# Lightning attention and a leaky-ReLU MLP on one core: the MLP begins on half a group of chunks, and one sum moves behind a drain

## The chip, the cores and the metric

The kernel runs on one core of a Trainium2 chip. A core has five engines with a queue each, which run beside one another and wait for one another through semaphores: TensorE (PE) multiplies matrices, VectorE (DVE), ScalarE (ACT) and GpSimd (POOL) work element by element, and SyncE (SP) issues the transfers. The metric is the time of the whole program on the device in microseconds; smaller is better.

## The reference

Two parts follow one another, all in float32 except the weights, which arrive as float64.

```python
for b in range(nb):                          # 12 blocks of 64 tokens, per batch (4) and head (8), head size 64
    intra = einsum('bhic,bhjc->bhij', qb, kb) * Dmask
    intra = einsum('bhij,bhjd->bhid', intra, vb)
    inter = einsum('bhid,bhde->bhie', qb * lam_pow, kv_state)
    out[:, :, sl] = intra + inter
    kv_state = lam_block * kv_state + einsum('bhsd,bhse->bhde', kb * rev_pow, vb)
...
x = out.transpose(0, 2, 1, 3).reshape(3072, 512)
h = x @ w_in                                 # 512 x 2048
g = maximum(0.01 * h, h)
return g @ w_out                             # 2048 x 512
```

The first part is attention with a decay per head: `intra` is what the tokens of a block give one another, `inter` is what the running state of all earlier blocks gives them. The second part is an MLP with a leaky ReLU.

## The kernel before

**Chunks.** Attention works on 24 chunks of 128 tokens (two blocks of 64). A chunk goes through `step()` (L473), which returns three parts; `c` is the new chunk and `b` the one before it:

1. `own(b)`: the `intra` rows of chunk `b` into the PSUM tile `po`; `inter(b, 0)`: half of its `inter` products, added in `po`.
2. `transpose_k`, `transpose_q` (L375, L382): PE transposes, ACT copies them out (L372), POOL multiplies the keys by their decay (L379), and the queries are multiplied as well, by DVE while the flag `alone` is set and by POOL later.
3. `scores(c)` into the PSUM tile `ps` (L391), `inter(b, 1)` (the other half), after which ACT writes chunk `b`, times 4, into the MLP's input `x` (L471); `kv(c)` and `sums_kv(c)` bring the state forward (L406, L422). While `alone` is set, `kv` uses the PSUM banks Z and W, later the banks of the transposes.

The two halves of `inter` are apart[...]; the scores stand between them.

**Groups and units.** Four chunks make a group of 512 tokens (six groups). The MLP works on a group in four units of 512 hidden columns: `up(g, u)` (L553) makes the hidden values, `down(g, u)` (L585) adds their share to the group's output `os`. Each is a product of 2 x 2 blocks done with seven multiplications instead of eight, in the manner of Strassen: `product` (L496) runs P1, P2, P6, P5, P7, P3, P4 in this order, alternately into the PSUM banks Z and W. Z stays open from P1 to P6, P7 and P4, W from P2 on: each bank gathers several products, and between them `keep` (L512: a copy on ACT, or an addition on DVE at L514 where the output already holds an earlier unit) and `total` (L518) drain it. A product that follows in a bank waits for that drain.

`PROD` (L491) says which blocks a product multiplies. A11 and A12 are the rows of a group's first two chunks, A21 and A22 those of its last two. S1 to S4 are sums of them: P6 uses S2, P5 S1, P7 S3 and P3 S4; P1 uses A11 and P2 A12 alone. `sums` (L535) makes them: for `x` of the first group on DVE, of later groups on POOL (`x_sums`, L545, called once all parts of a group's last `up` are out), and for the hidden values on DVE. There S1, S2, S3 are made at the end of `up` (L577), and S4 within `down`, after P2 has read A12, whose place it takes (L598). S3 takes the place of A21.

**Weights.** `conversion` (L244) turns each pair of float64 blocks into a float32 tile of seven slots, the four blocks and three differences T1, T2, T4 that the seven products need. ACT makes three passes for each block (L270, L281, L284), DVE two for a pair and one for each block (L289, L293, L298), and the differences (L305) are made by DVE or POOL, as `T_DVE` says by the pair's number. A raw block waits in the place of a weight tile that is not yet in use.

**What sets the order.** All engines' orders are written out by the Python program, which keeps a clock of its own per engine (`run`, L176), with a cost for each operation. Conversions stand in the lists `later` and are put into an engine's queue where the planned time has room for them (`emit`, L188); `need` (L199) forces those that the next unit requires. Loads are issued by SP in the order of the string `LOADS` (L160, `c` a chunk, `w` a weight block), as far as their places are free. `together(parts, n)` (L617) spreads the next `n` parts of attention over the products of a unit; the list `STEPS` has the `n` of each unit and `FIRST` how many parts run before the first one.

So before the first unit, 16 parts run: chunks 0 to 4 up to `own(4)` and its first half of `inter`.

Of the kernel before, what the change touches and what calls it, by code (L numbers as in the profile page):

```python
# [38 lines left out]
F32 = mybir.dt.float32  # L39
# [5 lines left out]
ALU = mybir.AluOpType  # L45
# [14 lines left out]
def kernel(  # L60
# [10 lines left out]
    nc = tc.nc  # L71
    P = 128
    B, H, S, D = q.shape
    C = P
    C2 = C // 2
    NCB = S // C
    HP = H // 2
    d_model, d_ff = moe_w_in.shape
    KO = d_model // P
    FO = d_ff // P  # L80
    NCH = B * NCB
    GC = 4
    NG = NCH // GC
# [4 lines left out]
    NU = NP // UP  # L88
# [68 lines left out]
    ROOMS = ["st"] + [f"{w}{p}" for w, p, h in reversed(blocks) if h == 0 and p >= UP]  # L157


    LOADS = "cwwcwwcwccccwwwcwwwccwwwwwwcwwwwwwwwwwwwwww" + "c" * NCH  # L160
    SLACK, AHEAD = (0.55, 0), (8.0, 14.0)

    T_DVE = [1, 3, 4, 9, 11, 14]

    FIRST, STEPS = 16, [4, 1, 2, 5, 6, 5, 3, 4, 0, 0, 0, 2, 0, 0, 0, 4]
    rooms = {}
    w_raw, lo, w_done = {}, {}, 0

# [7 lines left out]
    def run(eng, us, fn, after=(), gives=None, fill=True):  # L176
        t = max([ready.get(k, 0.0) for k in after], default=0.0)
        if fill and eng in later:
            while later[eng] and emit(eng, t + SLACK[alone]):
                pass  # L180
        clk[eng] = max(clk[eng], t) + us
        fn()
        if gives is not None:
            ready[gives] = clk[eng] + 0.1
        if eng != "DMA":
            pump()
# [22 lines left out]
    def pump(urgent=False):  # L209
        while urgent or clk["DMA"] < clk["PE"] + AHEAD[fin > 3]:  # L210
            able = [x for x in sorted(y[0] for y in loads.values() if y) if x[2]()]
            if not able:
                return
            loads[able[0][1]].pop(0)
            able[0][3]()
# [131 lines left out]
    def quad(out, rows, lhsT, rhs, cols, start=False):  # L347

        nc.tensor.matmul(out[HALF[cols]], lhsT=lhsT[HALF[rows]], rhs=rhs[HALF[rows]], start=start, stop=True,  # L351
                         skip_group_check=True)

    def tokens(t):
        return slice(t * C2, (t + 1) * C2)
# [94 lines left out]
        fin = b + 1  # L450
        ready["fin", b] = ready["own", b]

    def inter(b, n):


        def go():
            for i in range(HP):
                t = i % 2 ^ n
                for hi in range(2):
                    if b % NCB or t:  # L460
                        x, y = place(2 * i + hi)
                        quad(po[b][:, t, i, :], x, state[(2 * b + t - 1) % 4][:, y, :], qsT[b][:, y, tokens(t)], hi)

        run("PE", 0.3, go, [("qsT", b), ("state", 2 * b)], "inter")
        if n == 0:
            return
        g, r, t = b // GC, b % GC * C // T, b % GC * C % T
        if g not in X:
            X[g] = xp.tile([P, 2, 2, KO // 2, T], F32, name="x", tag="x", bufs=NX)
        x = X[g][:, r, :, :, t:t + C].rearrange("p h k (t i) -> p t (h k) i", t=2)  # L470
        run("ACT", 0.6, lambda: nc.scalar.mul(x, po.pop(b)[:, :, 0:HP, :], 4.0), ["inter"], ("x", b))  # L471

    def step():  # L473


        nonlocal at
        s, at = at, at + 1
        b, c = (x if 0 <= x < NCH else None for x in (s - 1, s))

        def has(x, *fs):  # L480
            for f in fs if x is not None else ():
                f(x)

        return [lambda: has(b, own, lambda b: inter(b, 0)),
                lambda: has(c, transpose_k, transpose_q),
                lambda: (has(c, scores), has(b, lambda b: inter(b, 1)), has(c, kv, sums_kv))]

    A = ("A11", "A12", "A21", "A22", "S1", "S2", "S3", "S4")  # L490
# [44 lines left out]
    def sums(eng, us, t, names, after):  # L535

        for o, a, b, op in (("S1", "A21", "A22", ALU.add), ("S2", "S1", "A11", ALU.subtract),
                            ("S3", "A11", "A21", ALU.subtract), ("S4", "A12", "S2", ALU.subtract)):
            if o in names:
                e = nc.vector if eng == "DVE" else nc.gpsimd  # L540
                run(eng, us, lambda: e.tensor_tensor(t[o], t[a], t[b], op=op), after, ("sum", eng, o))  # L541

    summed = set()

    def x_sums(g):  # L545
        summed.add(g)
        x = X[g]
        xs = xp.tile([P, 4, KO // 2, T], F32, name="xs", tag="xs")
        X[g] = {s: x[:, i // 2, i % 2] if i < 4 else xs[:, i - 4] for i, s in enumerate(A)}
        sums("DVE" if g == 0 else "POOL", 1.8 if g else 0.72, {s: x.rearrange("p k c -> p (k c)") for s, x in X[g].items()},  # L550
             A[4:], [("x", GC * g + GC - 1)])

    def up(g, u):  # L553
        q4 = ("A11", "A12", "A21", "A22")

        def begin():
            if g not in summed:
                x_sums(g)

            G[g, u] = {s: xp.tile([P, UP, T], F32, name=f"g{s}", tag=f"g{s}") for s in A[:6]}  # L560
            G[g, u].update(S3=G[g, u]["A21"], S4=G[g, u]["A12"])

        def mm(t, name, first):
            sa, sb = PROD[name]
            x = X[g][sa]
            for i in range(UP):
                w = WI[UP * u + i][:, SI[sb], :].rearrange("p (k f) -> p k f", k=2)
                for kk in range(2):
                    nc.tensor.matmul(t[:, i, :], lhsT=w[:, kk, :], rhs=x[:, kk, :],  # L569
                                     start=(first and i == 0 and kk == 0), stop=(i == UP - 1 and kk == 1),  # L570
                                     skip_group_check=True)

        def done(i):
            if i != 2:
                leaky(G[g, u][q4[i]], G[g, u][q4[i]], f"tot{i}", q4[i])
            else:
                sums("DVE", 0.72, G[g, u], ("S1", "S2", "S3"), ["A21", "A22", "A11"])  # L577

        parts = product(mm, 1.73, lambda i: G[g, u][q4[i]], lambda z: leaky(G[g, u]["A21"], z, "Z", "A21"), done,
                        lambda name: [("sum", "POOL" if g else "DVE", PROD[name][0]), ("x", GC * g + GC - 1)])  # L580
        return [lambda: (begin(), parts[0]())] + parts[1:]

    osb = {}
# [1 line left out]
    def down(g, u):  # L585
        def o(i):
            if g not in osb:
                osb[g] = tp.tile([P, GC, d_model], F32, name="os", tag="os", bufs=1)
            return osb[g][:, i // 2 * 2:i // 2 * 2 + 2, i % 2 * HD:(i % 2 + 1) * HD]

        def mm(t, name, first):
            sa, sb = PROD[name]
            for m in range(T // P):
                for i in range(UP):
                    nc.tensor.matmul(t[:, m, :], lhsT=G[g, u][sa][:, i, m * P:(m + 1) * P], rhs=WO[UP * u + i][:, SO[sb], :],  # L595
                                     start=(first and m == 0 and i == 0), stop=(i == UP - 1), skip_group_check=True)
            if name == "P2":
                sums("DVE", 0.72, G[g, u], ("S4",), ["W"])  # L598

        def put(z):  # L600
            if u == 0:
                run("ACT", 0.6, lambda: nc.scalar.copy(o(2), z), ["Z"])
            else:
                run("DVE", 0.72, lambda: nc.vector.tensor_tensor(o(2), o(2), z, op=ALU.add), ["Z"])

        def done(i):
            if u == NU - 1:
                rows = out[(g * GC + i // 2 * 2) * C:(g * GC + i // 2 * 2 + 2) * C, i % 2 * HD:(i % 2 + 1) * HD]
                nc.sync.dma_start(out=rows.rearrange("(m p) n -> p m n", p=P), in_=o(i))

        return product(mm, 1.73, o, put, done,
                       lambda name: [PROD[name][0], ("sum", "DVE", PROD[name][0])], u > 0)
# [4 lines left out]
    def together(parts, n):  # L617

        extra = []
        while len(extra) < n and (todo or at < NCH + 1):  # L620
            todo.extend([] if todo else step())
            extra.append(todo.pop(0))
        m = len(extra)
        for i, part in enumerate(parts):
            part()
            while m - len(extra) < m * (i + 1) // len(parts):
                extra.pop(0)()
        for x in extra:
            x()
# [4 lines left out]
    for i, x in enumerate(LOADS):  # L634
# [5 lines left out]
        else:  # L640
            loads[x].append((i, x, lambda n=n: room_free(n), lambda n=n: load_w(n)))
    pump()
    together([], FIRST)
    alone = False
    for n, (g, u, w) in enumerate((g, u, w) for g in range(NG) for u in range(NU) for w in range(2)):
        need((2 * u + w + 1) * NW // (2 * NU))
        together((up, down)[w](g, u), STEPS[n] if n < len(STEPS) else 3 * (w == 0))
        if (u, w) == (NU - 1, 0) and ("x", GC * g + 2 * GC - 1) in ready:
            x_sums(g + 1)

# [29 lines left out]
```

## Time and profile before

706.91 us, median of three runs (706.82 to 708.93). The profiled execution spans 707.5 us.

| engine | busy us | share of the span |
|---|---|---|
| PE (products) | 680.1 | 96% |
| PE (weight loads, beside the products) | 584.5 | 83% |
| DVE | 329.9 | 47% |
| ACT | 217.4 | 31% |
| POOL | 147.6 | 21% |

Where PE was not busy, us of each stretch:

| stretch | length | PE busy |
|---|---|---|
| 0 to 20 | 20.0 | 15.4 |
| 20 to 40 | 20.0 | 12.4 |
| 40 to 180 | 140.0 | 135.0 |
| 180 to 500 | 320.0 | 316.0 |
| 500 to 600 | 100.0 | 97.8 |
| 600 to 680 | 80.0 | 80.0 |
| 680 to 707.5 | 27.5 | 23.6 |

A line of a timeline gives start, duration, engine, source line, operation, output and inputs, number of instructions, and in brackets the idle time before it and what ended that. A product of the MLP shows as eight matrix instructions that start 1.73 us after those of the product before; it is drawn as 1.89 us long, since the ends overlap. In a line of windows, the busy time and number of instructions of PE, of its weight loads, of DVE, ACT and POOL follow one another, then the granted clock of PE (1.00 is full), the share of the DMA engines that was busy and what they moved.

### The profile page before, as it was taken

The numbers are of one execution on the slowest core, as the hardware profiler recorded it, in microseconds if no ns is written. First come the engines' busy times: TensorE is split into PE (matmuls) and PEld (weight loads), VectorE is DVE, ScalarE is ACT, GpSimd is POOL, SyncE is SP. The second block draws the span as 40 slices with busy tenths as digits, with TensorE's granted clock in tenths as the row PEclk, the third lists the DMA queues.
The fourth block names the chain that finished last, engine by engine and source line by source line (L and its number), as shares of the span: only waits on it lengthen the run. The fifth ranks groups of instructions, "written<-read, shape, count | busy, mean of one in ns | idle before, by whom it ended". The sixth has DMA issues, their size and how long they took to land.

```text
span 707.5 us, 13346 instructions
## 1 busy us (share of the span) xinstructions
PE 680.1 (96%) x5834; PEld 584.5 (83%) x5834; DVE 329.9 (47%) x488; ACT 217.4 (31%) x361; POOL 147.6 (21%) x141
## 2 busy tenths in 40 slices
PE   7689998999999999999999999999999998999997
PEld 5578777888888887888887888888888887888886
DVE  4768699876325325224245333343333244234324
ACT  4647767661221211321202223112122211221210
POOL 2741576557001004101205102103000003000000
PEclk9989999999999999999999999999999999999999
DMA  8998165643101003302202110000100000100001
GB/s 220 244 265 272 47 194 137 164 128 97 31 1 31 1 1 90 76 1 45 45 1 47 50 41 2 0 2 0 60 1 0 1 1 15 45 0 1 1 0 60
DMA packets 93130, 42.81 MB, mean 61 GB/s; under 512 B 76688, under 2 KB 91024, under 8 KB 93072
## 3 DMA queue, kind: packets, MB, share of 16 engines
q1 hardware_dynamic: 92928, 41.95, 22.5%
q8 instruction: 46, 0.75, 0.5%
q14 instruction: 12, 0.10, 0.0%
q10 hardware_dynamic: 144, 0.00, 0.0%
HBM read 35.66 MB, written 6.29 MB: 59 GB/s over the span
## 4 chain that ended last, share of the span: by engine, by line
PE 86%; DVE 6%; issue 2%; POOL 2%; ACT 1%; SPq 1%; DMA 1%; DVEq 0%; POOLq 0%; ACTq 0%
PE Z L595 23%; PE Z L569 23%; PE W L569 17%; PE W L595 16%; PE po L351 2%; PE pt L367 2%; PE ps L351 2%; DVE gS L541 2%; PE pu L351 1%; POOL state L433 1%; SPq L340 1%; POOL wi L305 1%; DMA q<-in_q_dram 1%; DVE state L430 1%; DVE os L514 1%
## 5 line engine op out<-in xcount | busy, mean ns | idle before, releaser
L595 PE MATMUL Z<-wo,gA 128*128 128x256 f32 x576 | 137.4, 381 | 0.0
L595 PEld LDWEIGHTS Z<-wo,gA 128*128 128x128 f32 x576 | 107.9, 190 | 14.8
L569 PE MATMUL Z<-x,wi 128*128 128x256 f32 x384 | 94.0, 387 | 1.1 <-DVE wi L298 0.5
L569 PE MATMUL Z<-xs,wi 128*128 128x256 f32 x384 | 91.3, 380 | 1.2 <-POOL wi L305 1.2
L569 PE MATMUL W<-xs,wi 128*128 128x256 f32 x384 | 91.7, 382 | 0.0
L516 ACT COPY gA<-Z 128x512 f32<-128x512 f32 x48 | 28.1, 585 | 206.5 <-PE Z L569 206.5
L595 PE MATMUL W<-wo,gA 128*128 128x256 f32 x384 | 90.8, 379 | 0.0
L569 PEld LDWEIGHTS Z<-x,wi 128*128 128x128 f32 x384 | 73.1, 193 | 12.3 <-DVE wi L298 1.4
L569 PEld LDWEIGHTS Z<-xs,wi 128*128 128x128 f32 x384 | 72.5, 190 | 11.4 <-POOL wi L305 1.6
L595 PEld LDWEIGHTS W<-wo,gA 128*128 128x128 f32 x384 | 72.8, 190 | 9.9
L569 PEld LDWEIGHTS W<-xs,wi 128*128 128x128 f32 x384 | 71.5, 190 | 9.6
L532 ACT ACTIVATE gA<-gA 128x512 f32<-128x512 f32 x72 | 45.3, 630 | 108.7 <-DVE gA L520 108.7
L520 DVE TENSOR_TENSOR gA<-gA,W 128x512 f32<-128x512 f32 x48 | 33.0, 688 | 88.0 <-PE W L569 84.6
L379 POOL TENSOR_TENSOR k<-k,decay 128x512 f32<-128x512 f32 (+1 forms) x24 | 27.2, 1133 | 216.0 <-PE pt L367 211.3
L520 DVE TENSOR_TENSOR gA<-gA,Z 128x512 f32<-128x512 f32 x24 | 16.5, 688 | 105.5 <-PE Z L569 105.5
L595 PE MATMUL Z<-wo,gS 128*128 128x256 f32 x192 | 48.3, 396 | 8.0 <-DVE os L514 8.0
L595 PEld LDWEIGHTS Z<-wo,gS 128*128 128x128 f32 x192 | 36.2, 194 | 16.3 <-DVE os L514 11.7
L541 POOL TENSOR_TENSOR xs<-x 128x512 f32<-128x512 f32 x10 | 14.9, 1493 | 156.0 <-PE W L569 156.0
L595 PE MATMUL W<-wo,gS 128*128 128x256 f32 x192 | 45.7, 381 | 0.0
L569 PE MATMUL W<-x,wi 128*128 128x256 f32 x192 | 45.6, 381 | 0.0
L433 POOL TENSOR_TENSOR state<-state,pow_q 128x256 f32<-128x256 f32 x40 | 30.8, 771 | 64.1 <-DVE state L430 44.7
L520 DVE TENSOR_TENSOR os<-os,W 128x512 f32<-128x512 f32 x48 | 32.8, 683 | 23.0 <-PE W L595 23.0
(76 smaller groups left out, 765.1 us busy)
## 6 DMA issues: line engine op xcount, KB each, us to landing
ws<-in_moe_w_in_dram SPq DMA_DIRECT2D x16, 512.0 KB, 5.5
ws<-in_moe_w_out_dram SPq DMA_DIRECT2D x16, 512.0 KB, 6.0
k<-in_k_dram SPq DMA_DIRECT2D x48, 128.0 KB, 4.1
q<-in_q_dram SPq DMA_DIRECT2D x48, 128.0 KB, 3.1
v<-in_v_dram SPq DMA_DIRECT2D x24, 256.0 KB, 4.0
out_dram<-os SPq DMA_DIRECT2D x24, 256.0 KB, 2.2
lam_b<-in_lam_dram ACTq DMA_DIRECT2D x1, 4.0 KB, 2.7
```

What stands on the lines that cost most here:

```text
L305: return lambda: e.tensor_tensor(*(W[p][:, s[i]:s[i] + m, :] for i in (out, a, b)), op=ALU.subtract)
L340: nc.sync.dma_start(out=x[:, i * HP:(i + 1) * HP, :], in_=y[i::2].rearrange("h p d -> p h d"))
L351: nc.tensor.matmul(out[HALF[cols]], lhsT=lhsT[HALF[rows]], rhs=rhs[HALF[rows]], start=start, stop=True, skip_group_check=True)
L367: nc.tensor.transpose(out=pt[:, y, :], in_=loaded[c][i][:, 2 * y:2 * y + 2, :].rearrange("p a d -> p (a d)"), identity=ident)
L379: run("POOL", 1.2, lambda: nc.gpsimd.tensor_tensor(kr[n], kr[n], _bc(pow_k, 3, D)[n], op=ALU.mult), [("pt", "k")], ("kd", c))
L433: run("POOL", 0.8, lambda: nc.gpsimd.tensor_tensor(state[(m + 1) % 4], new, _bc(lam_c, 2, D), op=ALU.mult), [("state", m)], ("lstate", m + 1))
L516: run("ACT", 0.6, lambda: nc.scalar.copy(dst(i), st[tag]), [tag], f"keep{i}")
L520: lambda: nc.vector.tensor_tensor(dst(i), dst(i), st[tag], op=ALU.add), [f"keep{i}", tag], f"tot{i}")
L532: run("ACT", 0.64, lambda: nc.scalar.activation(out=dst, in_=src, func=AF.Prelu, bias=0.0, scale=1.0, alpha=0.01), [after], gives)
L541: run(eng, us, lambda: e.tensor_tensor(t[o], t[a], t[b], op=op), after, ("sum", eng, o))
L569: nc.tensor.matmul(t[:, i, :], lhsT=w[:, kk, :], rhs=x[:, kk, :], start=(first and i == 0 and kk == 0), stop=(i == UP - 1 and kk == 1), sk ...
L595: nc.tensor.matmul(t[:, m, :], lhsT=G[g, u][sa][:, i, m * P:(m + 1) * P], rhs=WO[UP * u + i][:, SO[sb], :], start=(first and m == 0 and i ...
```

## The change

It has four parts.

- **The first unit begins on half a group.** P1 and P2 of the first `up` read the rows of chunks 0 and 1 alone. They now run between the parts of chunk 3: the program does nine parts, then takes three more one by one, with P1 behind chunk 3's transposes and P2 behind its scores and state. Both no longer wait for chunk 3's `x`. `FIRST` is 2 parts after this, where it was 16 in all. `alone` is cleared before chunk 3's `kv`, so that Z is free for P1.
- **Chunk 3's inter is made apart.** The sums of `x` need chunk 3 early. `early` runs `own(3)` and the first half of `inter` into `po`, and the second half at once into a tile in the place of the scores, `ps`, from which two additions on DVE bring it into `x`. So no scores of the next chunk need to stand between.
- **One sum of activations later.** S3 of the hidden values is made after P2 of `down` and the drain of its Z, with S4, and not at the end of `up`.
- **The last store in halves.** The last block of the output is added and stored in two halves.

With this go other values for the order of the loads (three weight blocks ahead of two chunks), for which differences DVE makes (pairs 0 and 7 join, 4 goes to POOL) and for how many parts of attention run beside each unit.

```diff
-    LOADS = "cwwcwwcwccccwwwcwwwccwwwwwwcwwwwwwwwwwwwwww" + "c" * NCH
+    LOADS = "cwwcwwcwccwwwcwwwccccwcwwwwwwwwwwwwwwwwwwww" + "c" * NCH
...
-    T_DVE = [1, 3, 4, 9, 11, 14]
+    T_DVE = [0, 1, 3, 7, 9, 11, 14]
-    FIRST, STEPS = 16, [4, 1, 2, 5, 6, 5, 3, 4, 0, 0, 0, 2, 0, 0, 0, 4]
+    FIRST, STEPS = 2, [3, 2, 1, 5, 4, 6, 3, 4, 0, 0, 1, 2, 0, 0, 0, 4]
...
-    def inter(b, n):
+    def inter(b, n, apart=False):
+        dst = pp.tile([P, 2, 2 * HP, C2], F32, name="ps", tag="ps") if apart else po[b]
...
-                        quad(po[b][:, t, i, :], x, state[(2 * b + t - 1) % 4][:, y, :], qsT[b][:, y, tokens(t)], hi)
+                        quad(dst[:, t, i, :], x, state[(2 * b + t - 1) % 4][:, y, :], qsT[b][:, y, tokens(t)], hi,
+                             start=apart and i < 2)
...
+        for t in range(2 if apart else 0):
+            y = x[:, t, 1 - t::2, :]
+            run("DVE", 0.45, lambda: nc.vector.scalar_tensor_tensor(y, dst[:, t, 1 - t:HP:2, :], 4.0, y, op0=ALU.mult,
+                                                                    op1=ALU.add), ["inter", ("x", b)], ("x", b))
...
+    def early(b):
+        own(b)
+        inter(b, 0)
+        inter(b, 1, apart=True)
...
-                sums("DVE", 0.72, G[g, u], ("S1", "S2", "S3"), ["A21", "A22", "A11"])
+                sums("DVE", 0.72, G[g, u], ("S1", "S2"), ["A21", "A22", "A11"])
...
             if name == "P2":
+                sums("DVE", 0.72, G[g, u], ("S3",), [])
                 sums("DVE", 0.72, G[g, u], ("S4",), ["W"])
...
+            for m in (slice(0, 1), slice(1, 2)) if last else (slice(0, 2),):
+                run("DVE", 0.72, lambda: nc.vector.tensor_tensor(o(2)[:, m], o(2)[:, m], z[:, m], op=ALU.add), ["Z"])
+                if last:
+                    store(2, m)
...
+    together([], 3 * GC - 3)
+    need(NW // (2 * NU))
+    parts, (own_2, whole_3, quads_3) = up(0, 0), step()
+    own_2()
+    whole_3()
+    alone = False
+    parts.pop(0)()
+    quads_3()
+    parts.pop(0)()
+    early(GC - 1)
+    x_sums(0)
     together([], FIRST)
-    alone = False
```

More of the change, by code (lines that the diff above doesn't have):

```diff
@@ L482, in has @@
                 f(x)
-        return [lambda: has(b, own, lambda b: inter(b, 0)),
+        old = b if b != GC - 1 else None
+        return [lambda: has(old, own, lambda b: inter(b, 0)),
                 lambda: has(c, transpose_k, transpose_q),
-                lambda: (has(c, scores), has(b, lambda b: inter(b, 1)), has(c, kv, sums_kv))]
+                lambda: (has(c, scores), has(old, lambda b: inter(b, 1)), has(c, kv, sums_kv))]
+    def early(b):
+        own(b)
+        inter(b, 0)
+        inter(b, 1, apart=True)
     A = ("A11", "A12", "A21", "A22", "S1", "S2", "S3", "S4")
@@ L541, in sums, with operand @@
                 run(eng, us, lambda: e.tensor_tensor(t[o], t[a], t[b], op=op), after, ("sum", eng, o))
-    summed = set()
+    XS = {}
+    def operand(g, s):
+        i = A.index(s)
+        return X[g][:, i // 2, i % 2] if i < 4 else XS[g][:, i - 4]
     def x_sums(g):
[L546 to L550, printed above, removed]
+        XS[g] = xp.tile([P, 4, KO // 2, T], F32, name="xs", tag="xs")
+        sums("DVE" if g == 0 else "POOL", 1.8 if g else 0.72, {s: operand(g, s).rearrange("p k c -> p (k c)") for s in A},
              A[4:], [("x", GC * g + GC - 1)])
@@ L556, in begin @@
         def begin():
-            if g not in summed:
+            if 0 < g not in XS:
                 x_sums(g)
@@ L564, in mm @@
             sa, sb = PROD[name]
-            x = X[g][sa]
+            x = operand(g, sa)
             for i in range(UP):
@@ L576, in done @@
             else:
-                sums("DVE", 0.72, G[g, u], ("S1", "S2", "S3"), ["A21", "A22", "A11"])
+                sums("DVE", 0.72, G[g, u], ("S1", "S2"), ["A21", "A22", "A11"])
         parts = product(mm, 1.73, lambda i: G[g, u][q4[i]], lambda z: leaky(G[g, u]["A21"], z, "Z", "A21"), done,
-                        lambda name: [("sum", "POOL" if g else "DVE", PROD[name][0]), ("x", GC * g + GC - 1)])
+                        lambda name: [("sum", "POOL" if g else "DVE", PROD[name][0]), ("x", GC * g + GC - 1 - 2 * (name in ("P1", "P2")))])
         return [lambda: (begin(), parts[0]())] + parts[1:]
@@ L602, in put, with store @@
                 run("ACT", 0.6, lambda: nc.scalar.copy(o(2), z), ["Z"])
-            else:
-                run("DVE", 0.72, lambda: nc.vector.tensor_tensor(o(2), o(2), z, op=ALU.add), ["Z"])
+                return
+            for m in (slice(0, 1), slice(1, 2)) if last else (slice(0, 2),):
+                run("DVE", 0.72, lambda: nc.vector.tensor_tensor(o(2)[:, m], o(2)[:, m], z[:, m], op=ALU.add), ["Z"])
+                if last:
+                    store(2, m)
+        last = (g, u) == (NG - 1, NU - 1)
+        def store(i, m=slice(0, 2)):
+            rows = out[(g * GC + i // 2 * 2) * C:(g * GC + i // 2 * 2 + 2) * C, i % 2 * HD:(i % 2 + 1) * HD]
+            nc.sync.dma_start(out=rows.rearrange("(m p) n -> p m n", p=P)[:, m], in_=o(i)[:, m])
         def done(i):
-            if u == NU - 1:
-                rows = out[(g * GC + i // 2 * 2) * C:(g * GC + i // 2 * 2 + 2) * C, i % 2 * HD:(i % 2 + 1) * HD]
-                nc.sync.dma_start(out=rows.rearrange("(m p) n -> p m n", p=P), in_=o(i))
+            if u == NU - 1 and not (last and i == 2):
+                store(i)
         return product(mm, 1.73, o, put, done,
@@ L642 @@
     pump()
+    together([], 3 * GC - 3)
[9 more added lines that the diff above has]
+    x_sums(0)
     together([], FIRST)
-    alone = False
     for n, (g, u, w) in enumerate((g, u, w) for g in range(NG) for u in range(NU) for w in range(2)):
         need((2 * u + w + 1) * NW // (2 * NU))
-        together((up, down)[w](g, u), STEPS[n] if n < len(STEPS) else 3 * (w == 0))
+        together((up, down)[w](g, u) if n else parts, STEPS[n] if n < len(STEPS) else 3 * (w == 0))
         if (u, w) == (NU - 1, 0) and ("x", GC * g + 2 * GC - 1) in ready:
```

## The prediction

> **What bounds the kernel now.** I read the page's busy shares first, then the waits of PE, then the timeline of each engine where PE stood still.
>
> ```profile
> PE 680.1 (96%) x5834; PEld 584.5 (83%) x5834; DVE 329.9 (47%) x488; ACT 217.4 (31%) x361; POOL 147.6 (21%) x141
> ```
>
> PE is busy for 680.1 of 707.5 us. The change takes no product away, so all it can win is PE's idle time (27.4 us) and the time in which PE ran at half clock. Waits of PE, total us, times, longest:
>
> ```profile
> PE Z L595 <- DVE os L514: 8.0, 6, 2.2
> PE ps L351 <- ACT qT L372: 5.1, 7, 1.1
> PE pu L351 <- issue: 2.8, 1, 2.8
> ...
> PE Z L569 <- POOL wi L305: 1.2, 1, 1.2
> ```
>
> The largest, 8.0 us, is `down`'s third product P6 waiting for the drain of its bank Z (`keep`, L514). The worst of the six, on DVE, POOL and PE:
>
> ```profile
> 590.93 0.95 DVE L541 TENSOR_TENSOR gS<-gA,gA 128x512 f32<-128x512 f32 x1 [1.67 <-ACT gA L532]
> 591.92 1.64 DVE L541 TENSOR_TENSOR gS<-gS,gA 128x512 f32<-128x512 f32 x1
> 593.48 1.75 DVE L541 TENSOR_TENSOR gA<-gA,gA 128x512 f32<-128x512 f32 x1
> 595.15 0.68 DVE L514 TENSOR_TENSOR os<-os,Z 128x512 f32<-128x512 f32 x1
> ...
> 592.98 1.70 POOL L541 TENSOR_TENSOR xs<-x,xs 128x512 f32<-128x512 f32 x1
> ...
> 591.83 1.89 PE L595 MATMUL W<-wo,gA 128*128 128x256 f32 x8
> 595.88 3.62 PE L595 MATMUL Z<-wo,gS 128*128 128x256 f32 x8 [2.16 <-DVE os L514]
> ```
>
> Three sums (S1, S2, S3) stand ahead of the drain on DVE, each slowed from 0.69 to as much as 1.75 us while POOL makes the next group's sums. P6 then takes 3.62 us where others take 1.89: the clock had dropped.
>
> The start, on PE, and then two 2-us windows (after the length and the five busy times stands PEclk, the granted clock, here 0.50 and 0.72):
>
> ```profile
> 33.44 0.53 PE L351 MATMUL pu<-v,k 64*64 64x64 f32 x24
> 36.73 0.48 PE L351 MATMUL pu<-v,k 64*64 64x64 f32 x6 [2.76 <-issue]
> ...
> 38.97 3.78 PE L569 MATMUL Z<-x,wi 128*128 128x256 f32 x8 [0.47 <-DVE state L430]
> ```
> ```profile
> 38.00:40.00 2.00, 1.53 (x22) 1.17 (x15) 1.48 (x3) 0.00 (x0) 1.46 (x2) 0.50 1.10 292
> 42.00:44.00 2.00, 2.00 (x8) 1.61 (x8) 0.00 (x0) 1.22 (x3) 0.00 (x0) 0.72 0.89 242
> ```
>
> The first product of the MLP starts at 38.97. Before it, PE works through attention alone with gaps, stands still for 2.76 us on nothing that the profile shows, and then runs P1 at half clock.
>
> **What the Trainium skill says.** "SBUF — State Buffer", Who interferes with whom: a VectorE instruction with two SBUF inputs contends with a GpSimd instruction that reads SBUF, and the later one blocks. The trace agrees: the sums (two SBUF inputs) take up to 1.75 us beside POOL and 0.69 without; the drain L514, which reads PSUM, spans 673 to 690 ns in all 54 cases. "TensorE: Matmul & The Clock Gate", What's actually happening: an idle window of about 3.4 us halves the clock. Here 2.76 and 2.16 us sufficed, 1.47 us (at 496) did not; the measurement decides. "DMA: Bandwidth & Descriptors", Anatomy of one DMA: about 2 us of fixed cost; stores of 256 KB land after a median of 2.2 us here.
>
> **The change, part by part.**
>
> *S3 after the drain.* In the changed order of DVE, L514 comes directly after S2, in each of the six groups. At 271, 387 and 496, S2 ends at 269.16, 384.75 and 494.13; the drain then ends about 0.65 later, at 269.8, 385.4, 494.8. PE was there at 270.3, 385.7 and 495.0 (start of P6 less its wait), so the waits of 1.21, 1.36 and 1.47 go. S3 now follows the drain, then S4, then the drain of W, for which P5 waits. S3 still overlaps POOL's last sum for 0.5 us, so it takes 1.0; with S4 and the drain at 0.6 each, W is free at 272.05, 387.5 and 497.0, where P5 could start at 272.05, 387.4 and 496.7. About 0.1, 0.2 and 0.35 comes back: gain 1.1 + 1.15 + 1.1. At 596, P6 can start at 594.25 instead of 595.88 and at full clock: with P5 held to 596.4, the next product starts at 598.2, where it started at 601.3 (595.88 + 3.62 + 1.79): gain 3.1. At 166, one sum (1.21) and three small operations stand between S2 and the drain; the new order has none: 1.0. In undisturbed units the drain only just comes late: P6 starts 0.05 late and lasts 1.88 instead of 1.73; seven such in the chain, 0.15 each: 1.0. Together 8.4; from 6.5 (without the small ones and with the clock dropping at 596 all the same) to 9.
>
> *P1, P2 ahead of chunks 2 and 3.* P1 needs the rows of chunks 0 and 1 (ACT has copied both by 23.2) and the weights of wi0 and wi1. DVE now makes wi0's three differences itself (T_DVE 0): 0.6 + 2 x 0.35, with POOL's key product beside them some 2 us, which moves the first part of wi1 (L298, 24.4 to 25.4 before) to about 26.6. PE ends chunk 3's transposes at 26.9, so P1 starts there, 12.1 us earlier. From then on PE, by hand with starts apart 1.73 a product, 0.5 each for ps, pu and own, 0.25 for half an inter and 0.87 for two transposes: P1 to 28.65; ps, inter, pu of chunk 3 to 29.9; P2 to 31.65; own, inter and the apart inter (8 pairs, 0.25) to 32.65; transposes of chunk 4 to 33.5. P6 needs S2, and that a new chain: P2 (31.65), DVE's add 32.35, leaky 33.0 (ahead of x on ACT), ACT's x of chunk 3 33.6, two DVE additions of 128x128, S1, S2. No row shows these additions; 128x512 takes 0.69 and 128x256 0.42, so 128x128 is 0.15 to 0.42; I take 0.28. S2 is ready at 35.5. PE stands for 2.0 us, and a half clock may follow. Then P6, P5 to 39.0; ps, pu of chunk 4, P7, P3, own, inter, P4: 46.0.
>
> Before, P4 ended at 56.64, with one chunk's transposes, ps, half inter, half pu and own more done (2.65): a lead of 8.0.
>
> *Then down(0,0).* Nine weight loads of 512 KB now stand before chunk 5 on the queue: 4.7 MB from 27.9 at 300 to 370 GB/s (what 44 to 58 us showed) is 13 to 16 us, so keys land about 44 to 47, and its transposes at 46 wait 0 to 1. ACT is what ends last: nine operations of conversion and copying stand before the drain of down's Z. From the leaky at 46.8, seven conversions of 0.55 to 0.72 and two copies of 0.48 end at 52.1; drain 52.65. PE had P2 done at 50.6, so P6 waits 2.1. With the drains behind it, up(0,1) starts at 63.3 (before: 71.02 with 2.2 more of chunk 6 done): the lead is 5.5. But conversions are now further ahead: wi3's differences are done on POOL by 63 (before, P6 at 77 waited 1.17 for them), and before, 71.02 to 87.08 held 13.7 of work: of the 2.35 lost I take back 2.0. Lead 7.5. Two gaps of 2.0 and 2.1 lie just under the 2.16 that halved the clock: some 1.5 to 1.8 each if they do; I take one, 1.5. Leaves **6.0**, bounds 2 and 9.
>
> *90 to 160 us.* Before, PE waits 0.78, 0.53, 1.05 and 0.37 here for DVE and ACT. T_DVE and the steps move these, and PE arrives earlier, but the conversions stand earlier in DVE's order too (when P2 of up(0,1) is drained, wo2 is done and wo3 half, where before wo2 had only begun). I count nothing.
>
> *Last store in halves.* The first half still waits for the whole product: the second addition has no wait of its own. DVE ends 703.65 + 0.42 + 0.35 instead of 704.34; the first half's issue (0.37) runs beside the second addition, the second store is of 128 KB: about 0.2, between -0.2 and 0.5.
>
> Sum: 8.4 + 6.0 + 0.2 = 14.6; 706.9 - 14.6 = **692.3**.
>
> **Rivals.** (a) *The start is given back.* The nine loads ahead of chunk 5, ACT's queue and two half clocks leave a lead of 1 and the sums bring 7.5: 698.4. For it: ACT's queue above, and PEclk 0.50 after 2.76 us of gap. Against: the gap at 34 and its half clock (5.5 us together) are passed over in any case. (b) *The waits between 90 and 125 go as well*, and no clock drops: 692.3 - 2.7 - 1.5 = 688.1. For it: the conversions' greater lead. Against: DVE is busy 18 of 20 us there. (c) *Slower.* PE starves in four of the first units for 3 us and each time runs 1.8 us at half clock (19.2), the lead is gone and the sums bring 8.4: 706.9 + 10.8 = 717.7. Against: conversions stand earlier, not later. (d) No change, the same with half the starvation (9.6 less 8.4: 708.1).
>
> **How the numbers follow.** Forecast 0.62, (a) 0.22, (b) 0.08, (c) 0.05, (d) 0.03. Range: forecast with its bounds (start 2 to 9, sums 6.5 to 9) 688.7 to 698.2, widened to most of (a) and (b): 687 to 700.5. Faster is the forecast with (a) and (b), 0.92; (c) gives slower; (d) same.
>
> **What would show it.** PE Z waiting for os L528 under 1.5 us in all, and no half clock at 596; P1's start near 27 and PEclk 1.0 at 36 to 44; a wait of 2 us ahead of the first sums' product, another at P6 of down(0,0) put down to ACT's copy; store landing unchanged. It is wrong if gaps for ACT, DVE or loads appear between 46 and 120, or if a second stretch at half clock does.

## The result, and the profile after

The changed kernel takes **702.1 us** (median of 4; 701.52 to 703.8), where the kernel before takes 706.87 beside it: ratio 0.9933, interval 0.9904 to 0.9962. It is faster by 4.8 us; 14.6 were forecast, and the time lies above the range. The profiled execution spans 702.0 us (before 707.5).

PE is busy for 677.3 us instead of 680.1 and idle for 24.7 instead of 27.4. Some waits went, and others came. Waits of PE after (what waits, for what: total us, times, longest):

```profile
PE Z L584 <- DVE xs L555: 3.0, 1, 3.0
...
PE W L610 <- DVE os L534: 2.3, 3, 1.7
...
PE Z L610 <- POOL qsT L388: 2.2, 1, 2.2
...
PE pu L351 <- DVE qsT L388: 1.7, 1, 1.7
...
PE Z L610 <- DVE os L528: 1.0, 2, 0.5
```

The last line is the wait that S3 was moved for: 8.0 us in six waits before, 1.0 in two after. The gap put down to "issue" (2.8) has left the list too. The first four lines are new, and the longest wait of each lies ahead of 65 us.

The end of the group at 590, DVE and then PE:

```profile
589.82 1.64 DVE L555 TENSOR_TENSOR gS<-gS,gA 128x512 f32<-128x512 f32 x1
591.38 0.67 DVE L528 TENSOR_TENSOR os<-os,Z 128x512 f32<-128x512 f32 x1
...
592.11 1.99 PE L610 MATMUL Z<-wo,gS 128*128 128x256 f32 x8 [0.49 <-DVE os L528]
594.39 1.99 PE L610 MATMUL W<-wo,gS 128*128 128x256 f32 x8 [0.28 <-DVE os L534]
```

The drain now directly follows S2. P6 waits 0.49 us instead of 2.16 and takes 1.99 instead of 3.62: the clock no longer drops.

The start, on PE, and then two 2-us windows (PEclk, the eighth number, is 0.61 and 0.50):

```profile
30.94 0.69 PE L351 MATMUL pu<-v,k 64*64 64x64 f32 x30 [1.67 <-DVE qsT L388]
31.56 2.94 PE L584 MATMUL W<-x,wi 128*128 128x256 f32 x8
...
40.24 3.78 PE L584 MATMUL Z<-xs,wi 128*128 128x256 f32 x8 [2.99 <-DVE xs L555]
43.81 3.03 PE L584 MATMUL W<-xs,wi 128*128 128x256 f32 x8
```
```profile
32.00:34.00 2.00, 2.00 (x8) 1.46 (x6) 0.58 (x2) 0.00 (x0) 1.23 (x2) 0.61 1.02 406
42.00:44.00 2.00, 2.00 (x6) 1.55 (x6) 1.39 (x2) 0.00 (x0) 0.00 (x0) 0.50 1.10 332
```

P1 started at 26.39, as forecast. Then PE waits twice, 1.67 and 2.99 us, and in this execution each time runs the following products at half clock: P2 in 2.94 us, P6 and P5 in 3.78 and 3.03, where full clock gives 1.73 to 1.99. Where the kernel before lost one stretch at half clock, the changed one has two. The first wait is for a PSUM bank and not for data: since `alone` is cleared earlier, chunk 3's state products (`pu`) go into the banks of the transposes, and DVE has yet to read the queries out of one of them (`qsT<-pt`, L388).

The first `down`, DVE, ACT and PE:

```profile
63.29 0.68 DVE L298 CUSTOM_DVE_ANT_0 wi<-wi,lo 128x1024 uint16<-128x1024 uint16 x1
63.89 0.68 DVE L534 TENSOR_TENSOR os<-os,W 128x512 f32<-128x512 f32 x1
...
60.24 0.58 ACT L530 COPY os<-Z 128x512 f32<-128x512 f32 x1
...
60.92 1.97 PE L610 MATMUL Z<-wo,gS 128*128 128x256 f32 x8 [2.23 <-POOL qsT L388]
64.63 1.99 PE L610 MATMUL W<-wo,gS 128*128 128x256 f32 x8 [1.74 <-DVE os L534]
```

Both drains come late. The trace names POOL as releaser of the first wait, but P6 starts 0.1 us after ACT's drain of Z ends (60.24 + 0.58); that drain stands behind conversions on ACT. The drain of W stands on DVE behind four conversions of the next weights, which run from 61.24 to 63.9.

### The profile page after: what moved, and what is told of

The parts are those of the page before. It is cut to its first block, busy times and chain, and to the rows that moved or that the text cites. A ratio compares the mean times of both kernels' runs of the same rounds, so it can differ in the third digit from the quotient of the medians.

```text
span 702.0 us, 13353 instructions
## 1 busy us (share of the span) xinstructions
PE 677.3 (96%) x5834; PEld 582.9 (83%) x5834; DVE 333.4 (47%) x493; ACT 217.5 (31%) x361; POOL 144.3 (21%) x139
## 4 chain that ended last, share of the span: by engine, by line
PE 87%; DVE 7%; POOL 1%; ACT 1%; DMA 1%; SPq 1%; issue 1%; DVEq 0%; ACTq 0%
PE Z L584 23%; PE Z L610 21%; PE W L584 18%; PE W L610 16%; PE po L351 3%; PE pt L367 2%; PE ps L351 2%; DVE gS L555 2%; PE pu L351 1%; DVE gA L555 1%; DVE wi L298 1%; POOL xs L555 1%; DMA q<-in_q_dram 1%; DVE wi L305 1%; SPq L340 1%
## 5 line engine op out<-in xcount | busy, mean ns | idle before, releaser
L584 PE MATMUL Z<-xs,wi 128*128 128x256 f32 x384 | 92.8, 385 | 3.0 <-DVE xs L555 3.0
L584 PE MATMUL Z<-x,wi 128*128 128x256 f32 x384 | 91.5, 381 | 0.9 <-DVE gA L534 0.9
L610 PE MATMUL Z<-wo,gS 128*128 128x256 f32 x192 | 46.0, 382 | 2.7 <-POOL qsT L388 2.2
L610 PEld LDWEIGHTS W<-wo,gS 128*128 128x128 f32 x192 | 35.8, 189 | 8.9 <-DVE os L534 4.1
L433 POOL TENSOR_TENSOR state<-state,pow_q 128x256 f32<-128x256 f32 x40 | 28.4, 709 | 69.0 <-DVE state L430 62.2
```

Of the source, the lines that this page charges most:

```text
L433: run("POOL", 0.8, lambda: nc.gpsimd.tensor_tensor(state[(m + 1) % 4], new, _bc(lam_c, 2, D), op=ALU.mult), [("state", m)], ("lstate", m + 1))
```

## The experiments

Each ratio is to the kernel before on the same chip; its interval is 95%.

### The sum alone, and the start alone

e1 is the kernel before with S3 moved; e2 is the changed kernel with S3 back in its old place, so it has the start and the halved store only.

```diff
 e1, on the kernel before (e2 undoes these two lines in the changed one)
-                sums("DVE", 0.72, G[g, u], ("S1", "S2", "S3"), ["A21", "A22", "A11"])
+                sums("DVE", 0.72, G[g, u], ("S1", "S2"), ["A21", "A22", "A11"])
...
+                sums("DVE", 0.72, G[g, u], ("S3",), [])
                 sums("DVE", 0.72, G[g, u], ("S4",), ["W"])
```

> The kernel before with S3 of the hidden values moved behind the drain, and nothing else. Theory A (the sum brings what was predicted, and the new start costs time): 706.9 - 8.4 = 698.5, that is faster than the whole change (702.1). Rival B (the sum brings only what the whole change shows, the start nothing): 702. Either way no half clock near 596 and PE's waits for L514 under 1.5 us in all.

> The changed kernel with S3 back at the end of up: the new start and the halved store alone. Theory A: slower than the kernel before by 3 to 4 us, about 710. Rival B: 707, no difference.

Measured: e1 701.52 us, 0.9908 (0.9887 to 0.9928), by the ratio 6.5 us less. e2 708.52 us, 1.0011 (0.9997 to 1.0026), no change. The move of one sum is the whole gain; start and store together bring nothing. The other values that were changed (loads, differences, numbers of parts) are in e2 together with the start, and no run tells them apart. The gain can be read off window by window (length, then PE's busy time). Before, and then e1:

```profile
180.00:300.00 120.00, 118.79 (x894) 103.09 (x893) 44.02 (x65) 28.40 (x48) 15.35 (x14) 1.00 0.13 32
400.00:500.00 100.00, 98.53 (x814) 85.13 (x813) 37.81 (x56) 23.62 (x41) 15.34 (x14) 1.00 0.06 19
500.00:600.00 100.00, 97.84 (x444) 85.04 (x443) 36.80 (x52) 19.34 (x32) 5.89 (x4) 0.98 0.03 11
```
```profile
180.00:300.00 120.00, 120.00 (x901) 104.42 (x900) 43.85 (x66) 28.39 (x48) 15.35 (x14) 1.00 0.13 34
400.00:500.00 100.00, 99.72 (x817) 86.01 (x816) 38.28 (x57) 22.59 (x40) 15.36 (x14) 1.00 0.07 20
500.00:600.00 100.00, 99.23 (x459) 86.71 (x458) 37.01 (x53) 19.32 (x32) 5.90 (x4) 1.00 0.04 14
```

Each group's end gives back 1.2 to 1.4 us of idle time (1.1 in the window 300 to 400, which isn't shown), and in the last PEclk goes from 0.98 to 1.00, two hundredths of 100 us, some 1.5 to 2 us: together about 6.5.

### Where the start's gain went: the clock

e3 lets PE run 24 idle transposes into an unused tile ahead of the first unit's P6, where it waits 2.99 us for the sums; e4 adds 14 more ahead of chunk 3's key-value products. They compute nothing that is used.

```diff
+    def fill(tag, n):
+        warm = pp.tile([P, 2 * P], F32, name="warm", tag=tag)
+        for _ in range(n):
+            nc.tensor.transpose(out=warm[:, 0:P], in_=ident, identity=ident)
...
     together([], FIRST)
+    fill("po", 24)
```

> The changed kernel with 24 idle transposes on PE between chunk 4's transposes and P6 of the first unit; they add work and no result. Theory C (the wait of 3.0 us ahead of P6 halves the clock, and that costs 3 us more): P6 and P5 take 1.9 us each instead of 3.8 and 3.0, and the total falls by about 3 us to 699. Rival D (DVE's and ACT's queues set the end of the first down, whatever PE's clock is): P6 and P5 are shorter but the first down waits longer, and the total stays at 701 to 702.

> The same, and 14 idle transposes more ahead of the kv products of chunk 3, where PE waits 1.7 us for DVE. Theory C: P2 too runs at full clock (1.9 us instead of 2.9), 4 to 5 us under the changed kernel, 697 to 698. Rival D: 701 to 702.

Measured: e3 699.35 us, 0.9873 (0.9851 to 0.9895); e4 700.88, 0.9897 (0.9875 to 0.9919). P6 and P5 in e3, and P6 of the first `down` in e4:

```profile
38.79 1.99 PE L584 MATMUL Z<-xs,wi 128*128 128x256 f32 x8 [0.28 <-DVE xs L555]
40.62 1.89 PE L584 MATMUL W<-xs,wi 128*128 128x256 f32 x8
```
```profile
56.71 3.40 PE L610 MATMUL Z<-wo,gS 128*128 128x256 f32 x8 [2.22 <-POOL qsT L388]
```

With PE kept at work, P6 and P5 run at full clock. The second `up` starts at 69.77 us instead of 74.11 in the changed kernel, and the span ends 4.3 us earlier (697.7): all of the lead was kept to the end. Not all of it is the idle work's. P6 starts 1.45 us earlier (38.79 against 40.24), since P2 ran at full clock in this execution (1.99 us), as it did in e2's without any idle work; the other 2.9 us are P6 and P5, as theory C had it. In e2's trace, with P2 at full clock and P6 at half, the second `up` starts at 72.72, 2.95 us later than in e3's. Idle work is thus worth more than the start itself, and e3 is the fastest version measured; its 4 runs (699.04 to 699.67) all lie under e1's 5 (701.14 to 702.97) on the same chip.

In e4, P6 of `down`, after a wait of 2.22 us, drops to half clock (3.40), which it had not done after 2.23 us in the changed kernel and in e3. That costs next to nothing there: the wait behind it shrinks from 1.73 to 0.29 us, and the second `up` starts at 69.91. P2 had run at full clock in e3's trace already, so that nothing more was to be won from it. The profiled executions of both are equally long (697.7 and 697.8); why e4's other four runs (700.75 to 701.35) are slower than e3's isn't shown.

### Where the start's gain went: queues

e5 moves P2 behind the early chunk's part and the sums, so that DVE and ACT can make the sums while PE works at P2. e6 takes the conversions away from in front of the first `down`'s two drains and of chunk 5's copies; they are done later. e7 is both. e11 is e5 again, beside e9 and e10.

```diff
 e5
     quads_3()
-    parts.pop(0)()
     early(GC - 1)
     x_sums(0)
+    parts.pop(0)()
 e6: fill=False for these runs
-        run("ACT", 0.6, lambda: nc.scalar.copy(into[c], pt), [("pt", nm)], (nm + "T", c))
+        run("ACT", 0.6, lambda: nc.scalar.copy(into[c], pt), [("pt", nm)], (nm + "T", c), fill=c != GC + 1)
...
-                run("ACT", 0.6, lambda: nc.scalar.copy(dst(i), st[tag]), [tag], f"keep{i}")
+                run("ACT", 0.6, lambda: nc.scalar.copy(dst(i), st[tag]), [tag], f"keep{i}", fill=fill or i != 0)
```

> The changed kernel with P2 of the first unit moved behind chunk 3's inter and the sums of x, so that it fills the time in which DVE makes S1 and S2. Theory C (the wait ahead of P6 and its half clock cost 5 to 6 us): the wait falls from 3.0 to under 1 us, P6 and P5 run at full clock, total 696 to 698. Rival D (later queues take it back): the first down waits longer and the total stays at 701 to 702.

> The changed kernel with no conversions put ahead of chunk 5's copies and of the two drains (keep 0, total 0) in the first down. Theory F (the seven conversions ahead of ACT's drain and the four ahead of DVE's cost PE the two waits of 2.2 and 1.7 us): both waits go, total 698 to 699. Rival G (the conversions are only late elsewhere): as much is waited for in the second up, total 701 to 702.

> Both of these edits together. Theories C and F: the gains add up, 693 to 695. Rivals D and G: 700 to 702.

> The kernel with the second product of the first unit moved behind the early chunk's part and the four sums, as measured at 714 us, repeated without other edits beside the others of this call, to have it on the same chip: 713 to 715 us.

Measured: e5 714.04 us, 1.0084 (1.0056 to 1.0111); e6 711.42, 1.0044 (1.0025 to 1.0063); e7 713.69, 1.0082 (1.0053 to 1.0111); e11 713.97, 1.0091 (1.0067 to 1.0115). e11 came as expected; e5, e6 and e7 missed: they are slower than the kernel before, where 696 to 699 us were expected of e5 and e6 and 693 to 695 of e7. The traces show a gain first and a larger loss later. In e5, P6 doesn't wait and P5 only 0.59 us, both at full clock, and the first unit's last product starts at 45.88 instead of 52.37: 6.5 us won. Two lines of its first `down` show what becomes of that:

```profile
52.80 2.87 PE L610 MATMUL Z<-wo,gA 128*128 128x256 f32 x6 [3.62 <-DVE wo L298]
...
61.81 2.53 PE L610 MATMUL W<-wo,gS 128*128 128x256 f32 x8 [2.31 <-DVE os L534]
```

PE is now ahead of the weights: it waits 3.62 us for the conversion of the second pair of output blocks (two of the product's eight instructions, which need the first pair alone, have run), and of 6.5 us 1.3 are left where the second `up` starts (72.84 against 74.11). In e6 the two waits of the first `down` shrink from 2.23 and 1.74 to 0.48 and 0.70, and the second `up` starts at 70.92, 3.2 us ahead. Both lose all that and more between 100 and 180 us, e6 mostly in one place:

```profile
166.09 2.93 PE L611 MATMUL Z<-wo,gA 128*128 128x256 f32 x6 [8.68 <-DVE wo L298]
```

The last output block's conversion is 8.68 us late. The changed kernel has no such wait.

### Why the later weights come late

In e5 and e6 a chunk's load had slipped ahead of a weight block on SP's queue. In e6 its q waits for a free tile until 84.18 us, and the weight load behind it issues at 85.75, where the changed kernel's issued at 73.36. e9 is the changed kernel with e6's order of loads and nothing else changed; e10 is e6 with the changed kernel's order of loads forced back; e12 is e10 with e3's idle transposes.

```diff
 e9
-            loads[x].append((i, x, lambda n=n: room_free(n), lambda n=n: load_w(n)))
+            loads[x].append((i, x, lambda n=n: len(loads["c"]) < NCH - {20: 8, 24: 10, 28: 11, 29: 12, 30: 13}.get(n, -1)
+                             and room_free(n), lambda n=n: load_w(n)))
 e10, on e6
-            loads[x].append((i, x, lambda n=n: n < fin + 3, lambda n=n: load(n)))
+            loads[x].append((i, x, lambda n=n: n < fin + 3 and (len(loads["w"])
+                             <= NW - {8: 21, 9: 24, 10: 26, 11: 29, 12: 30, 13: 31}.get(n, 0)), lambda n=n: load(n)))
```

> The changed kernel, with the weight blocks issued in the order that the two kernels with drains first and second product last had: four output blocks of the third unit behind the ninth chunk's load instead of one ahead of it, and the later ones shifted likewise. Nothing else is edited. Theory H (the whole loss of those two kernels comes from this order: a weight load queued behind a chunk's q load that waits for a free q buffer, so that all later conversions come some 10 us late): 709 to 712 us, with a wait of 5 to 9 us for the conversion of the last output block at about 160 us. Rival (the order alone is harmless, the loss came from the conversions that had been moved or from TensorE being ahead of the weights): 701.5 to 704 us and no wait over 2 us for the last output block.

> The kernel with drains first, with the order of the loads of the changed kernel forced back (a chunk's load waits in the planner until the weight blocks that stood ahead of it have been issued). Theories G and H (drains first saves some 3 us in the first down, which the slipped load order took back): first down's two waits of 2.2 and 1.7 us down to under 1.2 together as before, the second up starts at about 71 us instead of 74.1, and 698 to 700 us in all. Rival (with or without the order, conversions put off in the first down come back as a wait on weights later): 703 to 711 us, with over 3 us of waits on conversions between 100 and 180 us.

> Drains first with the forced load order, and the 24 idle transposes ahead of the first unit's third product. Theories C, G and H together: the gains add: 701 less 2 to 4 for the clock and less 3 for the drains, 694 to 697 us, and the second up starts at about 66.5 us. Rival D (what is gained at the start is waited away at the conversions of the later weights): 698 to 700 us, with the gain gone again by 180 us.

Measured: e9 709.47 us, 1.0029 (1.0016 to 1.0042); e10 710.78, 1.0038 (1.0026 to 1.005); e12 709.14, 1.0017 (1.0005 to 1.0029). The same place in e9, and then in e10:

```profile
163.20 2.93 PE L610 MATMUL Z<-wo,gA 128*128 128x256 f32 x6 [5.34 <-DVE wo L298]
```
```profile
164.19 2.93 PE L611 MATMUL Z<-wo,gA 128*128 128x256 f32 x6 [8.69 <-DVE wo L298]
```

The order of loads alone costs some 7 us (1.0029 against 0.9933), 5.34 of them in one wait. But it isn't the only cause: e10 has the old order back and waits as long as e6. Conversions that are put off in the first `down` come back as a wait at the last block, with or without the slipped loads. The rival named ahead of e10 holds; that e6's loss was only the loads falls.

Three more runs asked whether the place of the conversions in the in-order queues decides. e13 lets each drain pass the conversions in front of it but emits them directly behind it, with the changed kernel's order of loads; e14 is e5 with that order of loads (but for one chunk's load, which still goes out one weight block earlier); e15 is e13 with e3's idle transposes.

```diff
 e13, in run(); asked for by fill="behind" on the runs that e6 changes
+        if fill == "behind":
+            room = max(0.0, t + SLACK[alone] - clk[eng])
+            run(eng, us, fn, after, gives, fill=False)
+            room += clk[eng]
+            while later[eng] and emit(eng, room):
+                pass
+            return
```

> The changed kernel with the drains of the first down (and the fifth chunk's two transposes' copies) ahead of the conversions that used to stand before them, which now follow at once behind (they are not put off to a later place), and with the changed kernel's order of loads. In ScalarE's queue 64 drains and copies then stand ahead of the last block's last conversion, against 63 in the changed kernel and 69 in the three kernels that were slow. Theory K (the place of the conversions in the in-order queues, not the load order by itself nor TensorE's lead, decides whether the last output block is late): no wait over 2.5 us for it at about 160 us, first down's waits under 1.5 us together, 698 to 700.5 us. Rival L (whatever TensorE gains ahead of the second up, the conversions can't follow and it is waited away): over 4 us of waits for conversions between 100 and 180 us, 703 to 711 us.

> The second product of the first unit behind the early chunk's part and the four sums, now with the changed kernel's order of loads: 64 drains ahead of the last block's last conversion in ScalarE's queue, against 69 without it. Theory K: the 5.3 us wait for the last output block shrinks to under 2.5, and 712 to 714 us become 704 to 708 (the 3.6 us wait for the first output block stays). Rival L: 710 to 714 us as before.

> The kernel of the first run of this call with the 24 idle transposes ahead of the first unit's third product. Theory K: the two gains add, 694 to 697 us. Rival L: 699 to 710 us, with waits for conversions of 4 us or more between 100 and 180 us.

Measured: e13 711.51 us, 1.0059 (1.0038 to 1.008); e14 713.15, 1.0097 (1.0066 to 1.0128); e15 710.19, 1.0035 (1.0017 to 1.0054). Theory K falls as it was put. In all three the wait at the last block is still 4.75 us, now at P6, and the products of q and k wait for ACT's copy of q, which stands behind conversions that wait themselves. In e13:

```profile
135.11 0.69 PE L358 MATMUL ps<-qT,kT 64*64 64x64 f32 x32 [2.28 <-ACT qT L379]
...
170.59 2.93 PE L620 MATMUL Z<-wo,gS 128*128 128x256 f32 x6 [4.75 <-POOL wo L312]
```

Rival L, that a lead can never be kept, falls by e3: with DVE's and ACT's queues in exactly the changed kernel's order, a lead of 4.3 us at 70 us is still there at the end. What stays open is which feature of the interleaving decides. Every edit that let the planner place loads or conversions anew ended 6 to 12 us above the changed kernel (by the ratios); no run here finds an order that keeps both gains.

### The gap put down to "issue"

e8 is e1 with 26 instead of 10 idle transposes at the very start of PE's stream (`WARM = 26`): 16 more transposes.

> The kernel before with the later sum and 16 more idle transposes at the very start of PE, which have no part in the result. It asks what the gap of 2.8 us in chunk 4's kv products is, which comes after 24 of 32 and is put down to nothing. If it hangs on the place in PE's instruction stream (fetching of instructions), it comes 16 products earlier, after 8 of 32. If it is a wait for data or for another engine, it stays after 24, or goes. Total within 2 us of 701.

Measured: one run, 701.85 us. The gap in e1, with a window that ends inside it, and the same in e8 (in a window: length, then PE and weight loads with their counts):

```profile
37.31 0.34 PE L351 MATMUL pu<-v,k 64*64 64x64 f32 x8 [2.90 <-issue]
...
0.00:37.20 37.20, 25.38 (x602) 20.48 (x603) 22.97 (x46) 21.77 (x34) 16.62 (x24) 0.86 0.95 227
```
```profile
35.78 0.91 PE L351 MATMUL pu<-v,k 64*64 64x64 f32 x22 [2.53 <-issue]
...
0.00:34.20 34.20, 24.69 (x602) 20.66 (x603) 21.11 (x46) 19.56 (x31) 17.17 (x24) 0.85 0.99 235
```

The gap moved from behind 24 of 32 products to behind 8 of them, by the 16 transposes that were put in front, and stands after 602 matmuls and 603 weight loads in both. So no data are waited for: it hangs on the place in the instruction stream. That fits a refill of PE's instructions, and the traces hold its packet. A queue of its own brings 46 packets of 16 KB in the kernel before (`q8 instruction` among the DMA queues of its profile, 0.75 MB); by an estimate from these figures that is 65 bytes for each of PE's 11,668 products and weight loads, so it is taken for PE's. In the kernel before, e1 and e8 one of them starts at 34.16, 34.51 and 33.36 us, 0.1 to 0.2 us after PE fell idle, and takes 1.1 to 1.2 us; PE goes on 1.3 to 1.7 us after its end. It comes late: since the packet before it PE had started 428 to 488 products and loads, where over the whole run a packet comes for every 256 or so. The Trainium skill, "Runtime: NRT & Kernel Launch", Instruction fetch mechanics, says that an engine's instructions are streamed in blocks over a DMA queue of its own and that the cost of crossing a block is mostly hidden; here 2.5 to 2.9 us are not hidden, while all 16 transfer engines are near fully busy (DMA share 0.95 and 0.99 in the windows above). Why this packet comes late is shown in no run.

## Why the prediction was wrong, step by step

- **S3 after the drain: mechanism right, size 6.5 instead of 8.4 by the ratio.** The traces show the terms, from the start of P1 to the start of P7 in each of the 24 `down`s, e1 against before. The four group ends give 1.13, 1.12, 1.11 and 2.81 (6.2; forecast 6.45), and seven undisturbed units 0.15 each (1.1; forecast 1.0). The term at 166 (1.0) did not come: in e1 three small operations still stand ahead of the drain, and the unit takes 0.16 longer; in the changed kernel attention covers the place, and the unit is as long as in e2. That makes 7.2; e1's trace was 0.9 behind when the first `down` began, so 6.3 of it reach the span. By the ratio it is 1.9 of the 9.8 us missed.
- **P1's start: right.** 26.39 against 26.9. The half clock and the "issue" gap at 34 went, as forecast.
- **From P1 to P4 of the first unit: the failed step.** Forecast end of P4 46.0; its last product ended at 54.2. Three terms make up the 8.2. P6 started at 40.24 instead of 35.5 (4.7): PE waited 1.67 us for DVE to read chunk 3's queries out of the transposes' bank, a wait that the forecast did not have, because wi0's and wi1's differences took 2.65 and 2.35 us on DVE beside POOL where the forecast had some 2 us for the first and did not slow the second; P2 and the attention behind it ran at half clock (in the executions of e2 and e3 they did not); and S1 and S2 took 1.29 and 1.65 us beside POOL, so that the wait for the sums was 2.99 instead of 2.0. P6 and P5 then ran at half clock, 6.5 us from start to start of what follows instead of 3.46 (3.1); the rest is 0.4. I had kept 1.5 us for one half clock behind waits "just under the 2.16 that halved the clock": there were two, and e3 shows what the larger one cost, 2.9 us. The prediction had named a second stretch at half clock as a sign that it is wrong.
- **down(0,0): half right.** The wait of 2.1 us behind ACT's conversions came as 2.23. The second one, 1.74 behind DVE's conversions, was not seen, though DVE's order showed it. From P4 to the second `up` it took 19.9 us instead of 17.3.
- **Lead of 6.0 after all: none.** By e2 the start with the store brings 0.8 us less than nothing, with an interval around no change. Rival (a) had the mechanism, "two half clocks leave a lead of 1 and the sums bring 7.5"; both of its figures were still high. The part of the forecast that conversions further ahead give time back was right and too small: in e2's trace the second `up` starts 1.7 us later than in the kernel before, with 2.2 us of chunk 6 still to do, and by the last product 3.4 of these 3.9 us are made up, where 2.0 were counted.
- **Would the lead have been worth 6 without the half clocks?** Only in part. e5 removes them and is 6.5 us ahead at P4, and the second pair of output blocks isn't converted until 52.8. So a forecast of 46.0 for P4 set PE ahead of its weights, which the forecast had not asked about.
- **Store in halves: as good as nothing, as forecast.** From the end of the last product to the end of the span it is 3.75 to 3.77 us in all 14 traces with the halved store, and 3.83 to 3.84 in the three without it (before, e1 and e8): 0.08 came of the 0.2.

## What to carry to other kernels

A small move in a queue, a sum behind a drain for which TensorE waits, may bring more than a rebuilt start; look first for the drain that stands behind work that nobody awaits yet. If a stage is started earlier, price each product on its new neighbours: elementwise work beside GpSimd, and every wait of 2 us or more as a likely stretch at half clock behind it, and ask when the weights for the stage after it are ready. Where idle TensorE can't be given useful work, idle products during the wait can pay; and where a planner interleaves conversions in in-order queues, compare the order of those queues and of the loads before trusting any local edit.

## What the runs showed of the hardware

- **Idle time within a fixed step halves the clock, not the length of a gap.** In each of the 17 traces all stretches at half clock start on one grid with a step of 3.41 us, from the first to the last, and last one, two or three steps (the one at the end of a trace is cut off). Where PE, from 3 to 690 us, at full clock, was idle for 2.03 us or more of a step, the next step was always at half clock; up to 1.38 us it was not, but for one step at 18 us in e8; between, both occur, and what decides there isn't shown. So the 2.22 us in e4, which lie in one step, halve it, and the 2.23 us in the changed kernel, split over two steps, do not. Steps of e4, and then of the changed kernel (PEclk stands ahead of the last two numbers):

```profile
53.66:57.07 3.41, 1.19 (x6) 0.75 (x5) 3.34 (x6) 2.95 (x6) 1.61 (x1) 1.00 0.93 301
57.07:60.48 3.41, 3.12 (x9) 1.96 (x7) 3.34 (x7) 0.70 (x2) 0.65 (x1) 0.50 0.99 192
```
```profile
56.35:59.76 3.41, 2.35 (x11) 1.71 (x9) 3.31 (x7) 3.41 (x7) 0.62 (x1) 1.00 0.95 192
59.76:63.17 3.41, 1.97 (x8) 1.44 (x8) 3.34 (x4) 1.06 (x3) 1.00 (x1) 1.00 0.92 267
63.17:66.59 3.42, 1.96 (x12) 1.48 (x12) 3.39 (x5) 2.58 (x5) 2.38 (x3) 1.00 0.71 236
```

  The bank's 1.67 us ahead of P2 lie in one step in the changed kernel and are split in e6, where P2 runs at full clock. The Trainium skill, "TensorE: Matmul & The Clock Gate", What's actually happening, speaks of a free-running window of activity of some 3.4 us, whose phase varies by run. The grid agrees with that; that a whole idle window is needed does not, since 2.03 us of one sufficed.
- **24 idle transposes (2.84 us of PE) keep the clock full** over a wait that else costs 2.99 us and then 3.1 us at half clock.
- **A SCALAR_TENSOR_TENSOR over 128x128 with one operand in PSUM takes 0.28 to 0.29 us** on DVE; the prediction had taken 0.28.
- **A late refill of instructions can stop PE for 2.5 to 2.9 us.** The stall stands after the same 602 matmuls and 603 weight loads in the kernel before, e1 and e8, and the 16 KB packet starts 0.1 to 0.2 us after PE has stopped.
